# Three rounds of maxima at a time over six PSUM banks, with 24 projection matmuls between, in an attention and MLP kernel

## The chip, the cores and the metric

The kernel runs on one core of a Trainium2 chip. The metric is the device time of one execution in microseconds (us). The median of three runs of the kernel before is 1689.69 us (1689.48 to 1690.15).

## The reference

The input is layer-normed, then goes through 32-head attention (head size 16, 2048 tokens) and through an MLP; the attention's output is multiplied by a gate made of the MLP's output, and the input is added.

```python
xn = (x - mean) / sqrt(var + 1e-5)              # (2048, 512), no scale or shift
q, k, v = split(xn @ wqkv)                       # 32 heads of 16
p = softmax(q @ k.T / 4)                         # per head, 2048 x 2048
s = concat(p @ v) @ wo
h = relu(xn @ w1 + b1) ** 2                      # 1792 wide
g = silu(h @ w2 + b2)
out = x + s * g
```

## The kernel before

All matrix work is done in a 32-bit form. Where full accuracy is wanted, each factor is split in a high and a low part, and three products (high-high, high-low, low-high) are added up in one PSUM bank; `terms3` lists them. A projection tile, 128 outputs by 512 tokens with 512 inputs, is therefore 4 x 3 = 12 matmuls into one bank.

**Softmax with a true maximum.** The row maximum of the scores is found in a pass of its own. `max_mm` (L280) multiplies a block of 128 queries by 512 keys of one head into a bank of the pool `pm`, and VectorE reduces the bank to one number per query (L296). A head has 16 features, kept as three split parts in 64 rows of the array: two heads lie side by side, lane j = 0 in the rows 0 to 63 and lane j = 1 in the rows 64 to 127, so a matmul of lane 0 and one of lane 1 can run at the same time. After 64 such maxima for a unit of 512 queries and four heads (`max_end`, L300), `shift` (L324) transposes the maxima on TensorE, VectorE negates and splits them, and they go by DMA through DRAM into spare rows of the query tile `qe`, from which the second pass of scores (`exp_mm`, L1117) subtracts them inside the matmul.

**Stages.** The kernel begins with layer norm, transposes and the first projections (`ln_stats` to `ln_low`, `qk_tile`, `v_tile`). Then comes the lead (L1085 to L1114): the maxima run 24 steps ahead of the main loop. Each of the `LEAD = 24` steps g has two rounds; a round is one maximum of each lane, followed by `pump(8)`, which issues the next eight matmuls of the projections still to do (`rest`). The last matmul of a projection tile issues at once what empties its bank: for a V tile, ScalarE copies it to `vt` (L951) and a DMA stores it; for a Q or K tile, ScalarE copies it to `raw` (L934, two buffers), GpSimd splits that into `hl` (L80 and L81, three buffers), and two DMAs store it (L902). The Q and K tiles of the first column block (m divisible by 4) are instead split by ScalarE and VectorE straight out of the bank (L86, L87). Along the way `max_end` issues loads of later query tiles; step 0 loads weights, step 3 splits them, step 16 loads V and the biases, and step 17 does the first `shift`.

Then comes the main loop of 512 slots (L1268 on). Each issues matmuls of the second score pass, of the maxima 24 steps on, of the MLP or output projection, and of probabilities times V. Slots 0 and 1 take the last projection tile in two halves of six matmuls; with slot 2 the MLP begins, whose first load, `load_xc` (L469), has to wait until the projections are done, because its buffer takes their place.

**PSUM.** Eight banks: `pe` has three (tile `se`: projection tiles before the loop, second-pass scores in it), `pm` three (`pm_t`: transposes, maxima), `pd` one (`pd_t`: MLP and output projection, and the last projection tile), `pv` one (`po`: probabilities times V, in the loop alone).

**Order.** The order on TensorE is that of the Python calls, and so it is for ScalarE, VectorE and GpSimd in the lead and the loop. In the lead a scheduler orders the DMA queue of SyncE; in the loop it too follows the calls.

Of the kernel before, what the change touches and what calls it, by code (L numbers as in the profile page):

```python
# [8 lines left out]
F32 = mybir.dt.float32  # L9
# [7 lines left out]
P = 128  # L17
# [10 lines left out]
LEAD = 24  # L28
# [11 lines left out]
def kernel(  # L40
# [35 lines left out]
    def split(dst, raw, hi_act=False, lo=None):  # L76
        if hi_act:
            nc.scalar.activation(dst[0], raw, AF.Copy)
        else:
            nc.gpsimd.tensor_scalar(dst[0], raw, 1.0, 0.0, op0=ALU.mult, op1=ALU.add)  # L80
        (lo or nc.gpsimd).tensor_tensor(  # L81
            dst[1], raw, dst[0].bitcast(F32), op=ALU.subtract
        )

    def split_psum(hi, lo, ps):
        nc.scalar.activation(hi, ps, AF.Copy)  # L86
        nc.vector.tensor_tensor(lo, ps, hi.bitcast(F32), op=ALU.subtract)  # L87
# [8 lines left out]
    with ExitStack() as ph:  # L96
        kp = ph.enter_context(tc.tile_pool(name="kp", bufs=1))
        sp = ph.enter_context(tc.tile_pool(name="asp", bufs=2))
        pe = ph.enter_context(tc.tile_pool(name="pe", bufs=3, space=PSUM))
        pm = ph.enter_context(tc.tile_pool(name="pm", bufs=3, space=PSUM))  # L100
        pd = ph.enter_context(tc.tile_pool(name="pd", bufs=1, space=PSUM))
        pv = ph.enter_context(tc.tile_pool(name="pv", bufs=1, space=PSUM))
# [80 lines left out]
        def later(n, fn):  # L183
            waiting.append((now[0] + n, fn))
# [92 lines left out]

        togo = {}

        def max_mm(g, j):  # L280
            u = g // 16
            qd = u // 4
            if u not in mxs:
                mxs[u] = sp.tile([P, 16, 4], F32, name="mx")
                for i in range(2):
                    togo[u, i] = [(p, qb, kc) for p in range(2) for qb in range(4) for kc in range(4)]
            p, qb, kc = togo[u, j].pop(0)
            ps = pm.tile([P, 512], F32, name="pm_t")
            nc.tensor.matmul(  # L289
                ps,  # L290
                qms[u][p][64 * j : 64 * j + 64, qb * P : (qb + 1) * P],
                kas[qd, p][64 * j : 64 * j + 64, kc * 512 : (kc + 1) * 512],
                start=True, stop=True,
            )
            c = (2 * p + j) * 4 + qb
            return nc.vector.tensor_reduce(  # L296
                mxs[u][:, c, kc : kc + 1], ps, axis=AX.X, op=ALU.max
            )
# [21 lines left out]
        def shift_due(g):  # L320
            if late and late[0][0] <= g:
                shift(late.pop(0)[1])

        def shift(u):  # L324
            pt = pm.tile([P, 512], F32, name="pm_t")
            nc.tensor.transpose(pt[:16, :P], mxs[u], ident)  # L326
            sh = sp.tile([16, 2, P], F32R, name="sh", bufs=1)
            nc.vector.tensor_scalar(sh[:, 0], pt[:16, :P], -1.0, None, op0=ALU.mult)
            nc.vector.scalar_tensor_tensor(
                sh[:, 1], pt[:16, :P], -1.0, sh[:, 0].bitcast(F32),  # L330
                op0=ALU.mult, op1=ALU.subtract,
            )
            def keep():
                for i in range(2):
                    nc.sync.dma_start(
                        sh_d[u][:, i, :].rearrange("h (b n) -> h b n", n=P),
                        sh[:, i, :].bitcast(F32),
                    )

            def back():  # L340
                for p in range(2):
                    for i in range(2):
                        shift_rows(u, p, i)

            if in_loop:
                later(1, keep)
                later(2, back)
            else:
                keep()
                back()  # L350
# [547 lines left out]
        def qk_store(m, c, hl):  # L898
            cs = slice(c * 512, (c + 1) * 512)
            dst = q_d[m] if m < 4 else k_d[m - 4]  # L900
            for i in range(2):
                nc.sync.dma_start(dst[i, :, cs], hl[:, i].bitcast(F32))  # L902

        def qk_terms(m, c, ps):
            wq, m0 = wq_cols(m)
            ms = slice(m0, m0 + P)
            xT = xTs[c]
            return terms3(ps, [
                (lambda a, q, ko=ko: wq[q, a, ko, ms], lambda b, q, ko=ko: xT[q, b, ko])
                for ko in range(KO)  # L910
            ])

        def qk_tile(m, c, last=False):
            ps = pd.tile([P, 512], F32, name="pd_t") if last else pe.tile([P, 512], F32, name="se")
            for out_, lh, rh, first_, last_ in qk_terms(m, c, ps):
                nc.tensor.matmul(out_, lh(slice(0, P)), rh(slice(0, P)), start=first_, stop=last_)  # L916
                if not last_:
                    yield
            if last:

                hl = pools["n"].tile([P, 2, 512], F32R, name="hl")
                raw = sp.tile([P, 512], F32, name="ot", bufs=1)
                nc.scalar.activation(raw, ps, AF.Copy)
                split((hl[:, 0], hl[:, 1]), raw)
                later(6, lambda: qk_store(m, c, hl))
                yield
                return
            if m % 4 == 0:
                hl = hlp.tile([P, 2, 512], F32R, name="hl")
                split_psum(hl[:, 0], hl[:, 1], ps)  # L930
            else:
                hl = hlp.tile([P, 2, 512], F32R, name="hl")
                raw = hlp.tile([P, 512], F32, name="raw", bufs=2)
                nc.scalar.activation(raw, ps, AF.Copy)  # L934
                split((hl[:, 0], hl[:, 1]), raw)
            qk_store(m, c, hl)
            yield

        def v_tile(c, tt):
            xT = xTs[c]  # L940
            ps = pe.tile([P, 512], F32, name="se")
            ts_ = slice(tt * P, (tt + 1) * P)
            for out_, lh, rh, first_, last_ in terms3(ps, [
                (lambda a, q, ko=ko: xT[q, a, ko, ts_], lambda b, q, ko=ko: wa_t[q, b, ko, 2 * P :])
                for ko in range(KO)
            ]):
                nc.tensor.matmul(out_, lh(slice(0, P)), rh(slice(0, P)), start=first_, stop=last_)  # L947
                if not last_:
                    yield
            vt = vts[(4 * c + tt) % NVT]  # L950
            nc.scalar.activation(  # L951
                vt[:, :, :DH], ps.rearrange("p (h d) -> p h d", d=DH), AF.Copy
            )
            nc.sync.dma_start(v_d[:, c * 4 + tt, :], vt.rearrange("p h d -> p (h d)"))
            yield
# [48 lines left out]
        def pump(n):  # L1004
            for _ in range(n):
                while True:
                    todo = ahead or rest
                    if not todo:
                        return
                    if next(todo[0], todo) is not todo:  # L1010
                        break
                    todo.pop(0)
# [69 lines left out]
        pump(83)  # L1082
        warm = const.tile([P, 1], F32, name="warm")
        nc.scalar.activation(warm, eps_t, AF.Exp)
        for g in range(LEAD):  # L1085
            shift_due(g)
            for j in range(2):
                max_mm(g, j)
            pump(8)
            for j in range(2):  # L1090
                max_mm(g, j)
            pump(8)
            max_end(g)
            if g == 0:
                raw_r = [load_w("wv", 3 * P, ((D + P, 3 * P),))]
            if g == 3:
                for ko in range(KO):
                    split_w(wr_t, ko, slice(3 * P, 6 * P), raw_r[0][:, ko])
                ln.close()
                pools["v"] = ph.enter_context(tc.tile_pool(name="vp", bufs=1))  # L1100
            if g == 12:
                s1.close()
                ep = ph.enter_context(tc.tile_pool(name="ep", bufs=1))
                rot["pt"] = [ep.tile([P, 512], F32, name=f"pt{i}") for i in range(NPT)]
                pools["n"] = ph.enter_context(tc.tile_pool(name="np", bufs=1))
            if g == 16:
                load_v(0)
                nc.sync.dma_start(b1_t, b1.rearrange("(fo p) -> p fo", p=P), allow_slow_non_contiguous=True)
                nc.sync.dma_start(b2_t, b2[None, :].to_broadcast([P, D]))
            if g % 2 and g < 16:  # L1110
                c, i = divmod(g // 2, 2)
                nc.sync.dma_start(
                    xn_d[i, :, :, c * 512 : (c + 1) * 512], xTs[c][:, i].bitcast(F32)
                )  # L1114
# [211 lines left out]
```

## Time and profile before

| | us |
|---|---|
| median of three runs | 1689.69 |
| the profiled execution | 1688.97 |
| its span, first to last instruction | 1687.2 |
| TensorE busy with matmuls | 1658.8 |
| VectorE, ScalarE, GpSimd busy | 1352.7, 1192.5, 520.3 |
| the lead, from the first maximum to the loop's first | 69.35 to 187.67 |

In the profile's rows PE is TensorE's matmuls and PEld its weight loads, DVE is VectorE, ACT ScalarE, POOL GpSimd, and SPq the DMA queue that SyncE issues. A row of the timeline gives the start, the duration, the engine, the line, the operation and tile with its shape and how many instructions were merged, and in square brackets how long the engine had idled and what ended that. The end of a matmul is modelled, and matmuls overlap, so the spacing of starts tells more than a duration.

### The profile page before, as it was taken

What the parts mean: (1) busy time and instruction counts of PE and PEld (TensorE: products, weight loads), DVE (VectorE), ACT (ScalarE), POOL (GpSimd) and SP (SyncE); (2) the same over time, 40 slices, a digit from 0 to 9 for tenths busy, and PEclk for the clock granted to TensorE, in tenths of its full rate; (3) what the DMA queues carried; (4) which work ended last, traced back from release to release, by engine and by line L of the source; (5) the groups of instructions that cost most, each with busy time, mean ns of one, the idle gap of its engine ahead of it and who ended that gap; (6) DMA issues with size and microseconds to landing.
All of it is one profiled execution on the core that took longest, in us unless ns stands there. A gap on an engine that the chain in (4) does not pass through costs nothing.

```text
span 1687.2 us, 35420 instructions
## 1 busy us (share of the span) xinstructions
PE 1658.8 (98%) x13312; PEld 944.1 (56%) x13312; DVE 1352.7 (80%) x2303; ACT 1192.5 (71%) x2354; POOL 520.3 (31%) x538
## 2 busy tenths in 40 slices
PE   6999999999999999999999999999999999999998
PEld 5766566556545655565566456555655565555533
DVE  6255688888888888888888888888888888887633
ACT  7221477777777777777777777777777777776675
POOL 4335566522212321231133113211321233134322
PEclk9999999999999999999999999999999999999999
DMA  7548566435333333433343334323533352157434
GB/s 282 176 142 267 169 202 185 116 84 141 88 89 95 113 83 99 107 98 82 101 118 86 80 93 143 95 69 103 139 77 86 88 141 60 42 187 222 123 113 138
DMA packets 156316, 207.73 MB, mean 123 GB/s; under 512 B 50993, under 2 KB 70961, under 8 KB 154609
## 3 DMA queue, kind: packets, MB, share of 16 engines
q1 hardware_dynamic: 156144, 205.46, 42.5%
q8 instruction: 105, 1.72, 0.4%
q14 instruction: 67, 0.54, 0.1%
HBM read 149.04 MB, written 56.08 MB: 122 GB/s over the span
## 4 chain that ended last, share of the span: by engine, by line
PE 96%; DVE 1%; DMA 1%; ACT 1%; SPq 0%; issue 0%; DVEq 0%; ACTq 0%
PE po L362 30%; PE pm_t L289 17%; PE pd_t L236 17%; PE se L1125 12%; PE pd_t L204 9%; PE se L916 5%; PE se L947 3%; DVE mx L296 1%; PE pm_t L1125 0%; PE pm_t L816 0%; PE pm_t L326 0%; DMA xt<-in_A_x_dram 0%; DMA xc<-xn_d 0%; ACT pt L1132 0%; DMA wm<-in_A_wqkv_dram 0%
## 5 line engine op out<-in xcount | busy, mean ns | idle before, releaser
L296 DVE TENSOR_REDUCE mx<-pm_t 128x1 f32<-128x512 f32 x2048 | 1275.1, 684 | 233.4 <-PE pm_t L289 135.7
L1132 ACT ACTIVATE pt<-se 128x512 f32<-128x512 f32 x1730 | 902.4, 610 | 257.4 <-PE se L1125 225.2
L289 PE MATMUL pm_t<-ka,qm 64*128 64x512 f32 x2048 | 796.8, 423 | 3.1 <-DVE mx L296 2.9
L1125 PE MATMUL se<-qe,ka 64*128 64x512 f32 x2000 | 686.4, 402 | 0.0
L362 PE MATMUL po<-pt,v 128*32 128x512 f32 x3556 | 545.1, 605 | 0.0
L289 PEld LDWEIGHTS pm_t<-ka,qm 64*128 64x128 f32 x2048 | 352.6, 184 | 276.9 <-DVE mx L296 251.4
L1125 PEld LDWEIGHTS se<-qe,ka 64*128 64x128 f32 x2000 | 339.7, 184 | 21.0 <-issue 5.7
L236 PEld LDWEIGHTS pd_t<-xc,w1s 64*128 64x128 f32 x2352 | 292.2, 187 | 82.3 <-issue 82.2
L236 PE MATMUL pd_t<-xc,w1s 64*128 64x256 f32 x2352 | 332.3, 288 | 0.0
L236 PE MATMUL pd_t<-w2t,hT 64*128 64x512 f32 x936 | 259.9, 410 | 0.0
L236 PEld LDWEIGHTS pd_t<-w2t,hT 64*128 64x128 f32 x936 | 156.0, 184 | 73.3 <-issue 65.4
L362 PE MATMUL po<-ex,v 128*32 128x512 f32 x540 | 192.3, 605 | 0.0
L1132 ACT ACTIVATE ex<-se 128x512 f32<-128x512 f32 x270 | 147.4, 613 | 36.5 <-PE se L1125 30.8
L362 PEld LDWEIGHTS po<-pt,v 128*32 128x32 f32 x3556 | 79.9, 108 | 132.8 <-issue 112.4
L536 POOL TENSOR_TENSOR r<-r 128x512 f32<-128x512 f32 x49 | 51.1, 1042 | 329.6 <-ACT r L533 329.6
L555 POOL TENSOR_TENSOR u<-u,b_t 128x512 f32<-128x512 f32 x16 | 20.6, 1290 | 307.6 <-ACT u L554 307.6
L204 PE MATMUL pd_t<-w2t,hT 64*128 64x512 f32 x408 | 105.6, 391 | 0.0
L400 POOL TENSOR_TENSOR ot<-ot,hl 128x512 f32<-128x512 f32 x30 | 38.6, 1286 | 184.1 <-DMA hl<-r_d 184.1
L204 PE MATMUL pd_t<-wot,oc 64*128 64x512 f32 x336 | 90.9, 407 | 2.6 <-DVE m L316 0.8
L204 PEld LDWEIGHTS pd_t<-wot,oc 64*128 64x128 f32 x336 | 58.8, 185 | 47.3 <-DVE mx L296 12.4
L204 PEld LDWEIGHTS pd_t<-w2t,hT 64*128 64x128 f32 x408 | 72.8, 184 | 9.2
L533 ACT ACTIVATE r<-pd_t,b_t 128x256 f32<-128x256 f32 x98 | 41.1, 471 | 50.3 <-PE pd_t L236 50.3
(115 smaller groups left out, 1113.9 us busy)
## 6 DMA issues: line engine op xcount, KB each, us to landing
w1s<-w_d SPq DMA_DIRECT2D x196, 256.0 KB
qm<-q_d SPq DMA_DIRECT2D x384, 32.0 KB
qe<-q_d SPq DMA_DIRECT2D x384, 32.0 KB
ka<-k_d SPq DMA_DIRECT2D x96, 128.0 KB
xn_d<-xT SPq DMA_DIRECT2D x8, 1024.0 KB
k_d<-hl SPq DMA_DIRECT2D x32, 256.0 KB
q_d<-hl SPq DMA_DIRECT2D x32, 256.0 KB
xc<-xn_d SPq DMA_DIRECT2D x16, 512.0 KB
```

The costliest lines, as they stand in the source:

```text
L204: mm = nc.tensor.matmul(out_, lh(r), rh(r), start=first_ and lane == 0, stop=last_ and lane == 1, skip_group_check=True,)
L236: mm = nc.tensor.matmul(out_, lh(r), rh(r), start=first_ and lane == 0, stop=last_ and lane == 1, skip_group_check=True,)
L289: nc.tensor.matmul(ps, qms[u][p][64 * j : 64 * j + 64, qb * P : (qb + 1) * P], kas[qd, p][64 * j : 64 * j + 64, kc * 512 : (kc + 1) * 512] ...
L296: return nc.vector.tensor_reduce(mxs[u][:, c, kc : kc + 1], ps, axis=AX.X, op=ALU.max)
L362: nc.tensor.matmul(po[32 * j : 32 * j + 32, :], vs[qd][:, (4 * kb + j) * VW : (4 * kb + j) * VW + 32], pts[j], start=(kb == 0), stop=(kb = ...
L400: nc.gpsimd.tensor_tensor(ot, ot, hl[:, 1].bitcast(F32), op=ALU.mult)
L533: nc.scalar.activation(r[:, i], ps[:, i * CW : (i + 1) * CW], AF.Relu, bias=b1_t[:, fo : fo + 1])
L536: nc.gpsimd.tensor_tensor(r, r, r, op=ALU.mult)
L916: nc.tensor.matmul(out_, lh(slice(0, P)), rh(slice(0, P)), start=first_, stop=last_)
L947: nc.tensor.matmul(out_, lh(slice(0, P)), rh(slice(0, P)), start=first_, stop=last_)
L1125: nc.tensor.matmul(se, kas[qd, j // 2][b : b + 64, kb * P : (kb + 1) * P], qes[u][j // 2][b : b + 64, :], start=True, stop=True,)
L1132: return nc.scalar.activation(pts[j], se, AF.Exp, scale=0.25)
```

## The change

In the lead the rounds are no longer followed by eight matmuls each. Three rounds (six maxima) follow each other, and after every third come 24 matmuls of the projections, which are two whole tiles. The maxima of lane 0 go to the banks of `pe`, those of lane 1 to the banks of `pm`, so that six banks are in use. The projection tiles of the lead alternate between the single bank of `pd` and the single bank of `pv`. The numbers of maxima, projection matmuls and transfers are the same. The 48 rounds and 384 projection matmuls thus make 16 groups. What a step issues at its end (`max_end` and the loads) now comes after its second round and, where a group ends there, after the 24 matmuls. The first `shift` falls before the second round of a group.

```diff
-        def max_mm(g, j):
+        def max_mm(g, j, bank=None):
...
-            ps = pm.tile([P, 512], F32, name="pm_t")
+            ps = pm.tile([P, 512], F32, name="pm_t") if bank is None else bank()
...
+        led = []
+
+        def qkv_bank():
+            if not led:
+                return pe.tile([P, 512], F32, name="se")
+            led.append(0)
+            if len(led) % 2:
+                return pv.tile([P, 512], F32, name="po")
+            return pd.tile([P, 512], F32, name="pd_t")
+
         def qk_tile(m, c, last=False):
-            ps = pd.tile([P, 512], F32, name="pd_t") if last else pe.tile([P, 512], F32, name="se")
+            ps = pd.tile([P, 512], F32, name="pd_t") if last else qkv_bank()
...
         def v_tile(c, tt):
-            ps = pe.tile([P, 512], F32, name="se")
+            ps = qkv_bank()
...
-        for g in range(LEAD):
-            shift_due(g)
+        led.append(0)
+
+        for rnd in range(2 * LEAD):
+            g = rnd // 2
+            if rnd % 2 == 0:
+                shift_due(g)
             for j in range(2):
-                max_mm(g, j)
-            pump(8)
-            for j in range(2):
-                max_mm(g, j)
-            pump(8)
+                max_mm(g, j, None if j else lambda: pe.tile([P, 512], F32, name="se"))
+            if rnd % 3 == 2:
+                pump(24)
+            if rnd % 2 == 0:
+                continue
             max_end(g)
```

## The prediction

> **What bounds the kernel now.** I read the page first: the engines' busy shares and the chain of work that ended last.
>
> ```profile
> PE 1658.8 (98%) x13312; PEld 944.1 (56%) x13312; DVE 1352.7 (80%) x2303; ACT 1192.5 (71%) x2354; POOL 520.3 (31%) x538
> PE 96%; DVE 1%; DMA 1%; ACT 1%; SPq 0%; issue 0%; DVEq 0%; ACTq 0%
> ```
>
> TensorE is busy for 98% of the span and makes 96% of the chain. A microsecond saved on it anywhere should reach the end, unless something not tied to it has to be waited for. The second view is the same chain cut to the start of the lead, the third TensorE's timeline early and late in the lead.
>
> ```profile
> 55.42 11.20 PE se L947 x48
> ```
> ```profile
> 69.35 0.50 PE L289 MATMUL pm_t<-ka,qm 64*128 64x512 f32 x2
> 69.78 2.13 PE L947 MATMUL se<-wa_t,xT 128*128 128x512 f32 x8
> 71.84 0.50 PE L289 MATMUL pm_t<-ka,qm 64*128 64x512 f32 x2
> 72.27 2.13 PE L947 MATMUL se<-wa_t,xT 128*128 128x512 f32 x8
> ```
> ```profile
> 131.26 0.51 PE L289 MATMUL pm_t<-ka,qm 64*128 64x512 f32 x2
> 131.70 2.08 PE L916 MATMUL se<-xT,wr_t 128*128 128x512 f32 x8
> 133.71 0.51 PE L289 MATMUL pm_t<-ka,qm 64*128 64x512 f32 x2
> 134.14 2.08 PE L916 MATMUL se<-xT,wr_t 128*128 128x512 f32 x8
> ```
>
> Projection matmuls on the full array stream at 11.20 / 48 = 0.233 us each. In the lead a round takes 133.71 - 131.26 = 2.45 us late and 71.84 - 69.35 = 2.49 us early: 0.43 to 0.44 from the pair of maxima to the next full matmul, and 2.01 (early 2.06) for eight matmuls that would stream in 8 x 0.233 = 1.87. Nothing in these rows is a wait for another engine; what a round costs beyond streaming is the change of the array from 128 rows to two lanes of 64 and back.
>
> What a pair costs without a change of shape is seen at the loop's first slots, where pairs (one maximum, one second-pass score, in the two lanes) follow each other:
>
> ```profile
> 187.67 0.49 PE L289 MATMUL pm_t<-ka,qm 64*128 64x512 f32 x1
> 187.67 0.50 PE L1125 MATMUL se<-qe,ka 64*128 64x512 f32 x1
> 188.00 0.39 PE L289 MATMUL pm_t<-ka,qm 64*128 64x512 f32 x1
> 188.01 0.39 PE L1125 MATMUL se<-qe,ka 64*128 64x512 f32 x1
> 188.33 1.66 PE L916 MATMUL pd_t<-xT,wr_t 128*128 128x512 f32 x6
> ...
> 197.12 0.49 PE L289 MATMUL pm_t<-ka,qm 64*128 64x512 f32 x1
> ...
> 197.45 0.40 PE L289 MATMUL pm_t<-ka,qm 64*128 64x512 f32 x1
> ...
> 197.69 0.39 PE L289 MATMUL pm_t<-ka,qm 64*128 64x512 f32 x1
> ```
>
> Two pairs between full matmuls take 188.33 - 187.67 = 0.66 us, against 0.43 for one; a third adds 197.69 - 197.45 = 0.24.
>
> **The change, part by part.**
>
> *Fewer changes of shape.* The counts stay: 96 maxima and 384 projection matmuls, the same reductions, copies, splits and DMAs. A group of three rounds should take 0.66 + 0.24 = 0.90 us for its pairs, and for its 24 matmuls 2.01 + 16 x 0.233 = 5.74 (early 5.79): 6.64 late, 6.69 early. Three rounds before take 7.35 and 7.47. The early rate holds for the tiles with the first weights, nine tiles or about five groups: 5 x 6.69 + 11 x 6.64 = 106.5 us for all 16. The lead before runs from 69.35 to 187.67, 118.3 us. The difference is 11.8 us.
>
> *The first group.* Its third lane-0 maximum takes the `pe` bank of the last projection tile before the lead, which VectorE still has to read:
>
> ```profile
> 70.09 0.69 DVE L87 TENSOR_TENSOR hl<-se,hl 128x512 fp32r<-128x512 f32 x1 [13.31 <-ACT hl L86]
> 70.69 1.28 DVE L296 TENSOR_REDUCE mx<-pm_t 128x1 f32<-128x512 f32 x2
> ```
>
> It can start at about 70.8, and would otherwise at 69.35 + 0.33 + 0.24 = 69.9: TensorE loses 0.9 us, once. The six reductions behind it, at 1.28 a pair, end at 70.69 + 3 x 1.28 = 74.5, before the second group at about 76.6.
>
> *The group with the shift.* Step 17 begins with the 35th round, the second of its group. Today the transpose costs little:
>
> ```profile
> 150.84 0.51 PE L289 MATMUL pm_t<-ka,qm 64*128 64x512 f32 x2
> 151.27 2.08 PE L916 MATMUL se<-xT,wr_t 128*128 128x512 f32 x8
> 153.19 0.27 PE L326 MATMUL pm_t<-ident,m 128*16 128x128 f32 x1
> 153.39 0.50 PE L289 MATMUL pm_t<-ka,qm 64*128 64x512 f32 x2
> ```
> ```profile
> 151.37 1.29 DVE L296 TENSOR_REDUCE mx<-pm_t 128x1 f32<-128x512 f32 x2 [1.16 <-PE pm_t L289]
> ```
>
> That round takes 153.39 - 150.84 = 2.55, 0.1 more than others. Now the transpose takes a fourth `pm` bank inside a group, so the third lane-1 maximum waits for the reduction of the first. A reduction starts 151.37 - 150.84 = 0.53 after its pair and two take 1.29: the bank is free 1.8 us after the group begins, when about 0.8 would have done. With the transpose's own change of shape I take 1.2 us, once; bounds 0.1 (as today) and 2.0.
>
> *VectorE.* Six reductions take 3 x 1.29 = 3.87 us, and with 0.53 ahead of them end 4.4 us after the group begins; the next begins at 6.64. TensorE's 24 matmuls hide them with 2 us to spare, so I cost the six banks at nothing.
>
> *Two banks for projections.* Instead of three `pe` banks there are one of `pd` and one of `po`. A bank is wanted again after one other tile and three rounds: 12 x 0.233 + 0.90 = 3.7 us after its tile's end. What empties it is ScalarE, then GpSimd and the stores:
>
> ```profile
> 187.86 0.60 ACT L934 ACTIVATE raw<-se 128x512 f32<-128x512 f32 x1 [2.75 <-PE se L916]
> ```
> ```profile
> 188.54 0.63 POOL L80 TENSOR_SCALAR hl<-raw 128x512 fp32r<-128x512 f32 x1 [1.36 <-ACT raw L934]
> 189.25 1.29 POOL L81 TENSOR_TENSOR hl<-raw,hl 128x512 fp32r<-128x512 f32 x1
> ```
>
> The lead's last tile gives way to the loop's first pair at 187.67, and its copy is done at 188.46: free 0.8 us after the tile, against 3.7. GpSimd needs 190.54 - 188.54 = 2.0 us a tile and gets 6.64 / 2 = 3.3. I cost it at nothing; if ScalarE's copy came later than 3.7 us after a tile, all of the excess would fall on TensorE. The DMAs are the same in number, 10% closer together; the moves of a few query loads past stores on SyncE's queue change nobody's due time by more than a few us, and those tiles are used tens of us later. ScalarE's split of weights at step 3 now comes ahead of another tile's copy and delays it by at most its own 1.75 us, within the same slack:
>
> ```profile
> 88.97 1.75 ACT L880 ACTIVATE wr_t<-wv 128x384 fp32r<-128x384 f32 x4
> ```
>
> *After the lead.* Slots 0 and 1 find all banks free, as the last 24 matmuls come after the last maxima. What is late next is the MLP's first load:
>
> ```profile
> 193.76 1.26 SPq L472 DMA_DIRECT2D xc<-xn_d  x2
> ```
> ```profile
> PEld pd_t L204 <- DMA xc<-xn_d: 0.4, 1, 0.4
> ```
>
> It is issued when the last projection matmul is over, so it moves with the lead; TensorE waits for it 0.4 us now, and with the last stores closer together that may grow by up to 1 us. The loop behind it is TensorE's, and inherits the earlier start whole.
>
> *Sum.* 118.3 - (106.5 + 0.9 + 1.2) = 9.7 us. The profiled execution, 1688.97 us (span 1687.2 and 1.8 around it), would become 1679.3; it lies 0.7 under the median of the runs, so 1680.0 in their terms. With neither one-off loss the gain is 11.8 (1677.9); with the shift at 2.0, 1 us more at the MLP's load, and 0.2 us a group lost on the pairs (the first rival below), it is 9.7 - 0.8 - 1.0 - 3.2 = 4.7 (1685.0).
>
> **The rivals.**
>
> *The pairs do not stream as in the loop* (the change does half of what it says). Two pairs of maxima could follow at the 0.33 us of 188.00 to 188.33 instead of 0.23. Against: 197.45 to 197.69. Cost 32 x 0.10 = 3.2 us: 1683.2.
>
> *The banks set the pace.* In the loop TensorE does wait for reductions:
>
> ```profile
> 190.50 0.39 PE L289 MATMUL pm_t<-ka,qm 64*128 64x512 f32 x1
> 191.20 0.49 PE L289 MATMUL pm_t<-ka,qm 64*128 64x512 f32 x1 [0.32 <-DVE mx L296]
> ```
>
> The start comes 0.70 after the one before it, 0.47 more than streaming. If each of 16 groups had such a wait, 7.5 of the 9.7 us would be gone: 1687.5, no measurable change. For it: six banks are filled in 0.9 us and emptied in 3.9. Against it: the 5.74 us of other work between. The loop packs four maxima on three banks into a slot, without that pause. [...]
>
> *Slower: the projection banks.* If the copy out of `pd` or `po` lagged, TensorE would stand before every tile. The lag would come from behind: `hl` has three buffers, whose stores must land, and at step 16 SyncE's queue is held by the loads of V and biases. The point is a lag of 3.7 us after a tile; to lose 9.7 and 3.4 more it must be 13.1 / 16 = 0.8 us beyond, 4.5 us in all groups. At 5.0 the loss is 16 x 1.3 = 20.8: 1700.8. For it: two banks, two `raw`, three `hl`. Against: ScalarE and GpSimd wait for TensorE in these rows (2.75 and 1.36 us idle), not the other way.
>
> **How the numbers follow.** 0.2% is 3.4 us, about what a measurement of this kernel can tell from no change. Forecast as summed, 0.75, own range 1677.9 to 1682.5; pairs that do not stream, 0.11; banks set the pace, 0.08; slower, 0.06. The first two lie over 0.2% below: faster 0.86. Same 0.08, slower 0.06. The range takes in the first two with the bounds above: 1677.9 to 1685.0.
>
> **What would show it.** In the changed kernel's timeline the lead starts at about 69.4 and its groups follow every 6.6 to 6.7 us; the pairs inside start 0.33 and 0.24 apart; the first group's third pair starts near 70.9; one group late in the lead has a wait for a reduction of about 1 us; the loop's first pair starts near 178. The prediction is wrong if TensorE shows waits for L296 or for L934 in every group, or if the first MLP matmul does not come about 9.5 us earlier than now:
>
> ```profile
> 200.16 0.78 PE L204 MATMUL pd_t<-xc,w1s 64*128 64x256 f32 x2
> ```

## The result and the profile after

The changed kernel takes 1678.51 us in the median of six runs (1677.46 to 1681.39), the kernel before 1689.92 us (1689.17 to 1692.16). The ratio is 0.9937, 95% interval 0.9925 to 0.9948: 11.4 us faster, 8.8 to 12.7 by the interval. The profiled execution of the changed kernel was the slowest of its six, 1681.39 us with a span of 1679.6.

The page of the changed kernel shows the same engines at the same shares, with 12.0 us less on TensorE's matmuls:

```profile
PE 1646.8 (98%) x13312; PEld 945.2 (56%) x13312; DVE 1350.0 (80%) x2303; ACT 1192.7 (71%) x2354; POOL 519.2 (31%) x538
```

TensorE's timeline shows the first group, the second, one late in the lead, and the loop's first pair (lines of this kernel lie 12 to 16 further down: L959 is the V tiles, L928 the Q and K tiles, L1141 the second pass of scores):

```profile
69.91 0.49 PE L289 MATMUL pm_t<-ka,qm 64*128 64x512 f32 x1
...
70.25 0.39 PE L289 MATMUL pm_t<-ka,qm 64*128 64x512 f32 x1
71.39 0.50 PE L289 MATMUL se<-ka,qm 64*128 64x512 f32 x1 [0.75 <-DVE hl L87]
...
71.82 3.06 PE L959 MATMUL pd_t<-wa_t,xT 128*128 128x512 f32 x12
74.71 2.97 PE L959 MATMUL po<-wa_t,xT 128*128 128x512 f32 x12
77.61 0.49 PE L289 MATMUL se<-ka,qm 64*128 64x512 f32 x1
...
77.95 0.39 PE L289 MATMUL se<-ka,qm 64*128 64x512 f32 x1
...
78.18 0.39 PE L289 MATMUL se<-ka,qm 64*128 64x512 f32 x1
...
78.50 3.06 PE L959 MATMUL pd_t<-wa_t,xT 128*128 128x512 f32 x12
```
```profile
151.57 0.49 PE L289 MATMUL se<-ka,qm 64*128 64x512 f32 x1
...
152.46 3.01 PE L928 MATMUL pd_t<-xT,wr_t 128*128 128x512 f32 x12
...
158.12 0.49 PE L289 MATMUL se<-ka,qm 64*128 64x512 f32 x1
...
177.78 0.49 PE L1141 MATMUL se<-qe,ka 64*128 64x512 f32 x1
...
190.27 0.52 PE L204 MATMUL pd_t<-xc,w1s 64*128 64x256 f32 x2
```

Three pairs and the return to the full array take 78.50 - 77.61 = 0.89 us, 24 matmuls 158.12 - 152.46 = 5.66, a late group 6.55. The lead takes 177.78 - 69.91 = 107.9 us in place of 118.3. In this execution it began 0.56 us later than in the one before, so the first MLP matmul comes 200.16 - 190.27 = 9.9 us earlier.

The weight loads (PEld) show one place where a change of shape costs. The first two rows below are of the kernel before, whose pair starts at 131.26 and whose next full matmul at 131.70; the other two are the second pair of the changed kernel's group at 151.57:

```profile
131.26 0.18 PEld L289 LDWEIGHTS pm_t<-ka,qm 64*128 64x128 f32 x2 [0.35 <-issue]
131.69 1.66 PEld L916 LDWEIGHTS se<-xT,wr_t 128*128 128x128 f32 x8 [0.25 <-issue]
```
```profile
151.67 0.19 PEld L289 LDWEIGHTS se<-ka,qm 64*128 64x128 f32 x1
...
151.90 0.39 PE L289 MATMUL se<-ka,qm 64*128 64x512 f32 x1
```

Between pairs the weights are loaded 0.23 us ahead, under the matmul before. At both edges of a pair in the kernel before, the load starts only with its own matmul. How much of the price of a change is this load, the rows do not show.

The place of each unit's transpose on TensorE (L326) tells how far the new execution is ahead of the old one along the loop. The second, the 30th and the 31st of the 32, in the kernel before and then in the changed one:

```profile
213.77 0.28 PE L326 MATMUL pm_t<-ident,m 128*16 128x128 f32 x1
...
1500.68 0.28 PE L326 MATMUL pm_t<-ident,m 128*16 128x128 f32 x1
...
1557.49 0.28 PE L326 MATMUL pm_t<-ident,m 128*16 128x128 f32 x1
```
```profile
203.58 0.28 PE L326 MATMUL pm_t<-ident,m 128*16 128x128 f32 x1
...
1490.19 0.28 PE L326 MATMUL pm_t<-ident,m 128*16 128x128 f32 x1
...
1550.38 0.28 PE L326 MATMUL pm_t<-ident,m 128*16 128x128 f32 x1
```

It is 10.2 us ahead, then 10.5, then 7.1. The 3.4 us are lost at one place, shown by VectorE's timeline and SyncE's queue around it:

```profile
1525.81 2.49 DVE L296 TENSOR_REDUCE mx<-pm_t 128x1 f32<-128x512 f32 x4 [0.83 <-PE pm_t L289]
1532.89 0.25 DVE L386 RECIPROCAL sm<-sm 128x16 f32<-128x16 f32 x1 [4.59 <-DMA sm<-ot]
```
```profile
1524.51 2.70 SPq L134 DMA_DIRECT2D qe<-q_d  x6
1527.26 0.42 SPq L743 DMA_DIRECT2D sp_d<-s  x1
1527.72 2.75 SPq L134 DMA_DIRECT2D qm<-q_d  x6
1530.89 0.62 SPq L380 DMA_DIRECT2D sm<-ot  x1
```

VectorE stands still for 4.59 us before the reciprocal of the softmax sums of a late unit, because the DMA that brings them waits on SyncE's queue behind twelve query loads (2.70 and 2.75 us for the two times six). TensorE then waits 2.96 us for the maxima's banks, before its matmul at 1533.74. The kernel before has this wait too, 2.38 us long in its profile. The change does not make it. The 3.4 us lost there are about what this one execution lies above the median (2.9 us).

### The profile page after: what moved, and what is told of

Read it like the earlier page. It is cut to its first block, busy times and chain, and to the rows that moved or that the text cites. A ratio compares the mean times of both kernels' runs of the same rounds, so it can differ in the third digit from the quotient of the medians.

```text
span 1679.6 us, 35423 instructions
## 1 busy us (share of the span) xinstructions
PE 1646.8 (98%) x13312; PEld 945.2 (56%) x13312; DVE 1350.0 (80%) x2303; ACT 1192.7 (71%) x2354; POOL 519.2 (31%) x538
## 5 line engine op out<-in xcount | busy, mean ns | idle before, releaser
L296 DVE TENSOR_REDUCE mx<-pm_t 128x1 f32<-128x512 f32 x2000 | 1246.1, 684 | 183.8 <-PE pm_t L289 85.9
L1141 PE MATMUL se<-qe,ka 64*128 64x512 f32 x2000 | 686.8, 402 | 0.0
L1141 PEld LDWEIGHTS se<-qe,ka 64*128 64x128 f32 x2000 | 340.0, 184 | 21.6 <-issue 5.7
```

The source lines that it names most:

```text
L296: return nc.vector.tensor_reduce(mxs[u][:, c, kc : kc + 1], ps, axis=AX.X, op=ALU.max)
L1141: nc.tensor.matmul(se, kas[qd, j // 2][b : b + 64, kb * P : (kb + 1) * P], qes[u][j // 2][b : b + 64, :], start=True, stop=True,)
```

## The experiments

The theory is that of the prediction: each change of the array from 128 rows to two lanes of 64 and back costs TensorE time, and grouping removes 32 of 48; the banks only let the grouped maxima and tiles go unhindered. The prediction's rows put the price of one change at 2.45 - 0.24 - 1.87 = 0.34 us late and 2.49 - 0.23 - 1.87 = 0.39 us early: a round of before, less a streaming pair and eight streaming matmuls. The rivals are that the banks themselves save the time, and that reductions or copies take it back.

### The changed kernel again

> The changed kernel once more, to stand beside the variants on the same chip. The theory (each change of the array between full rows and two lanes costs TensorE 0.34 to 0.39 us, and 32 of 48 are gone) expects the lead to take 107.9 us from the first maximum to the loop's first, as in the profile of the changed kernel, and the time to be 9.5 to 11.5 us below the kernel before. In that profile a wait of 3.0 us for a reduction near 1530 us stood behind a DMA that brings the softmax sums; if such waits come and go with the transfers, this profile has it at another length while the lead is the same within 0.5 us.

1678.89 us, ratio 0.9943 (0.9928 to 0.9958) to the kernel before (1690.21). The lead runs from 69.15 to 177.04, 107.89 us, the same to 0.1. VectorE's longest wait for the sums was 2.1 us in this profiled execution (1678.23 us). So the lead is steady. What differs between these two executions arises late in the loop: the 30th transpose starts at 1490.19 in the one and at 1489.90 in the other, the 31st at 1550.38 and 1546.44.

### Banks alone

```diff
-            if rnd % 3 == 2:
-                pump(24)
+            pump(8)
```

> The changed kernel's banks with the old order: one round, then eight projection matmuls. The theory (the order saves, the banks only make it possible) expects the lead at 118.3 us and the time of the kernel before, within 1 us. The rival (the banks save: lane 0 and lane 1 in different pools, projections apart from the maxima) expects 8 us or more below it.

1689.25 us, ratio 1.0003 (0.9993 to 1.0013). The lead takes 187.67 - 69.34 = 118.33 us, as before to 0.01. The banks save nothing by themselves, and with one round at a time projecting into two single banks costs nothing.

### Order alone

```diff
-                max_mm(g, j, None if j else lambda: pe.tile([P, 512], F32, name="se"))
+                max_mm(g, j)
...
-        led.append(0)
-
         for rnd in range(2 * LEAD):
```

> Three rounds at a time and 24 matmuls between, in the old banks: maxima on the three of pm, projections on the three of pe. The theory expects the fourth, fifth and sixth maximum of each group to wait for the reductions of the first three, which end 1.2, 1.85 and 2.5 us after the group begins: pairs take about 2.9 us instead of 0.9, 16 x 2.0 = 32 us lost against the changed kernel, so about 21 us above the kernel before (1703 to 1718). The rival that banks do not matter expects the changed kernel's time, 1678 to 1681.

1733.65 us (two runs, 1728.79 and 1738.51), ratio 1.0265 (1.0228 to 1.0301): 44 us above the kernel before, twice what was expected. The waits are there, but they cost only a part of it. TensorE's timeline of one group and the granted clock over its 24 matmuls:

```profile
101.83 0.73 PE L289 MATMUL pm_t<-ka,qm 64*128 64x512 f32 x3
103.11 1.70 PE L289 MATMUL pm_t<-ka,qm 64*128 64x512 f32 x3 [0.55 <-DVE mx L296]
104.74 7.41 PE L959 MATMUL se<-wa_t,xT 128*128 128x512 f32 x24
```
```profile
104.74:112.08 7.34, 7.34 (x25) 5.57 (x25) 1.30 (x3) 0.60 (x1) 0.00 (x0) 0.77 0.14 47
```

The six maxima take 104.74 - 101.83 = 2.91 us, as worked out. The 24 matmuls behind them, which wait for nothing, take 7.34 us in place of 5.78: the seventh number after the stretch, the granted clock, is 0.77 there. The lead takes 164.2 us, 56 more than the changed kernel's; the waits make 16 x 2.0 = 32 us of that, the slower matmuls about 16 x 1.6 = 25. So the six banks are a condition, and without them the order costs far more than it saves.

### Two rounds at a time

```diff
-            if rnd % 3 == 2:
-                pump(24)
+            if rnd % 2 == 1:
+                pump(16)
```

> Two rounds at a time and 16 projection matmuls between, in the changed kernel's banks: 24 groups in place of 16. By the theory a group takes 0.66 us for two pairs and 2.01 + 8 x 0.233 = 3.88 (early 3.93) for 16 matmuls, 4.54 to 4.59 us; the lead takes 24 of these, 109 to 110 us, and has neither of the two single losses (no third bank is wanted in the first group, no fourth in the group of the transpose). So it is 1.2 to 2.5 us behind the changed kernel, 8 to 9 us below the kernel before. The rival, that the other banks save the time, expects no difference to the changed kernel; a rival by which only whole tiles in a row save time expects much less than 8 us.

1680.20 us, ratio 0.9943 (0.9928 to 0.9958). The lead runs from 69.70 to 178.51, 108.81 us. That is 10.0 us below the kernel before, where 8 to 9 were expected. Against the changed kernel's 1678.89 in the same comparison the 1.3 us are as expected, but less than the spread of the runs; the conclusion rests on the lead's duration. It falls by (118.33 - 108.81) / 24 = 0.40 us for each change of shape that is gone. Sixteen matmuls are a tile and a third, so the saving does not need whole tiles in a row.

### Without the two single losses

```diff
-        pump(83)
+        pump(71)
+        led += [0, 0]
+        pump(12)
...
-        led.append(0)
...
-            if rnd % 2 == 0:
+            if rnd % 3 == 0:
                 shift_due(g)
```

> The changed kernel without its two single losses: the last projection tile before the lead goes to the bank of pv, so that the first group's third maximum finds a free bank, and the transpose is issued ahead of a group instead of after its first pair. The theory expects the lead at 106.0 to 106.6 us (107.9 less 0.75 to 0.9 for the first group and 0.6 to 0.9 for the transpose), and the time 1.4 to 2.0 us below the changed kernel. The rival, that these waits are covered by something later, expects no difference.

1677.80 us, ratio 0.9935 (0.9919 to 0.9950). The lead runs from 70.11 to 175.96, 105.85 us, 2.0 less than the changed kernel's; the first group has no wait:

```profile
70.11 0.49 PE L289 MATMUL se<-ka,qm 64*128 64x512 f32 x1
...
70.45 0.39 PE L289 MATMUL se<-ka,qm 64*128 64x512 f32 x1
...
70.68 0.39 PE L289 MATMUL se<-ka,qm 64*128 64x512 f32 x1
...
71.00 3.06 PE L959 MATMUL pd_t<-wa_t,xT 128*128 128x512 f32 x12
```

Of the 2.0 us, the first group gives 1.0 (6.67 in place of 7.70 us) and the group with the transpose 0.95 (7.04 in place of 7.99). That group is still 0.5 above the others: the transpose starts 0.20 us ahead of its first pair (149.25 and 149.45), it still takes a bank of `pm`, and the third maximum of lane 1 starts 0.18 us behind that of lane 0 (150.20 and 150.02). The transpose now also comes one group later, because the next group begins two rounds after it is due.

The median is 1.1 below the changed kernel's, which these runs cannot tell from nothing. With 48, 24 and 16 groups at 118.33, 108.81 and 105.85 us, the price of a change of shape is 0.40 and (108.81 - 105.85) / 8 = 0.37 us.

### Six rounds at a time

```diff
-            if rnd % 3 == 2:
-                pump(24)
+            if rnd % 6 == 5:
+                pump(48)
```

> Six rounds at a time and 48 projection matmuls between: twelve maxima over six banks, eight groups. Fewer changes of shape would save another 8 x 0.35 = 2.8 us, but from the seventh maximum on each waits for a reduction: the pairs of a group take about 4.85 us in place of 1.6, 8 x 3.25 = 26 us. The theory expects 20 to 26 us above the changed kernel (1699 to 1704). A rival by which reductions never hold TensorE expects 2 to 3 us below it.

1715.49 us (two runs), ratio 1.0157 (1.0137 to 1.0177): 37 us above the changed kernel's 1678.89 of the other comparison instead of 20 to 26. Again the waits are as worked out, and the clock falls on top:

```profile
104.31 0.49 PE L289 MATMUL se<-ka,qm 64*128 64x512 f32 x1
...
105.58 0.49 PE L289 MATMUL se<-ka,qm 64*128 64x512 f32 x1 [0.32 <-DVE mx L296]
106.18 0.49 PE L289 MATMUL pm_t<-ka,qm 64*128 64x512 f32 x1
106.82 0.47 PE L289 MATMUL se<-ka,qm 64*128 64x512 f32 x1 [0.15 <-DVE mx L296]
...
109.30 5.49 PE L959 MATMUL pd_t<-wa_t,xT 128*128 128x512 f32 x12
```
```profile
104.31:109.30 4.99, 4.21 (x14) 1.69 (x13) 4.46 (x8) 0.60 (x1) 0.00 (x0) 0.89 0.53 172
109.30:114.58 5.28, 5.28 (x13) 4.12 (x13) 2.81 (x5) 0.00 (x0) 0.00 (x0) 0.50 0.32 114
114.58:123.06 8.48, 8.48 (x37) 6.72 (x36) 0.00 (x0) 1.79 (x3) 3.77 (x4) 0.98 0.40 134
```

The maxima take 109.30 - 104.31 = 4.99 us (4.85 expected); the next twelve matmuls take 5.28 at a granted clock of 0.50, where twelve behind the pairs of the changed kernel's first group take 74.71 - 71.82 = 2.89 at a granted clock of 1.00. In two later groups these twelve take 4.44 us each (182.59 to 187.03, 200.00 to 204.44). Of the group sizes tried, three rounds are the largest with which six banks leave TensorE no wait in an ordinary group.

### One projection bank

```diff
-            if len(led) % 2:
-                return pv.tile([P, 512], F32, name="po")
             return pd.tile([P, 512], F32, name="pd_t")
```

> The changed kernel with all projection tiles of the lead in the one bank of pd. The second tile of each group has to wait for ScalarE's copy of the first (0.2 us to its start, 0.60 long, 0.1 until TensorE goes on), the first tile of the next group finds its bank emptied behind the 0.9 us of pairs. The theory expects 16 x 0.9 = 14 us more than the changed kernel, 1690 to 1695, and thereby that the second bank hides all of that copy. If the copies lag by several us (the slower rival of the prediction), it expects 16 x 3 us or more, over 1720; if the banks are no limit, no change.

1697.53 us (two runs), ratio 1.0051 (1.0031 to 1.0071): 18.6 us above the changed kernel's 1678.89 of the other comparison, against 14 expected.

```profile
131.90 0.49 PE L289 MATMUL se<-ka,qm 64*128 64x512 f32 x1
...
132.79 3.01 PE L926 MATMUL pd_t<-xT,wr_t 128*128 128x512 f32 x12
136.57 3.02 PE L926 MATMUL pd_t<-xT,wr_t 128*128 128x512 f32 x12 [0.77 <-ACT raw L944]
139.52 0.49 PE L289 MATMUL se<-ka,qm 64*128 64x512 f32 x1
```

A group takes 139.52 - 131.90 = 7.62 us in place of 6.55, so one uncovered copy costs 1.07 us, not 0.9. The tile after the pairs does not wait. In the changed kernel neither tile waits, so the second bank hides the copy whole; copies that lag by several us are not there.

### The sums one slot later

In addition to the edits of the variant without the single losses:

```diff
-EVAC_LAST = (1, 3, 4, 5, 7, 9)
+EVAC_LAST = (1, 4, 4, 5, 7, 9)
```

> As the variant without the two single losses, and in addition the reciprocal of the softmax sums of the last four units (EVAC_LAST) is issued one slot later, so that VectorE has one slot of 3.3 us more before it meets the DMA that brings the sums. If the 3.0 us by which the changed kernel's profiled execution fell behind near 1530 us is VectorE standing in that wait, the profile here shows no wait over 1 us there, and the time is 1 to 4 us below the variant without this edit, with a smaller spread. If the wait comes from elsewhere, nothing changes.

1674.78 us (1673.47 to 1675.89), ratio 0.9913 (0.9897 to 0.9929). All its five runs lie below all six of the variant without this edit (1676.12 to 1681.61), 3.0 us in the medians, and the spread falls from 5.5 to 2.4 us. The wait for the sums, 2.8 us once late in the loop in that variant's profile, is gone there. Who waited, from 1450 to 1670 us, first without the edit and then with it:

```profile
DVE sm L386 <- DMA sm<-ot: 2.8, 1, 2.8
PE pm_t L289 <- DVE mx L296: 1.8, 3, 1.2
```
```profile
PE pm_t L289 <- DVE mx L296: 0.6, 2, 0.3
```

The transposes on either side of that place show what it is worth in the profiled executions: the one with the edit is 1.0 us ahead at the 30th (1488.14 against 1489.15) and 3.0 ahead at the 31st (1543.39 against 1546.40), so 2.0 us are gained there. The spans differ by only 0.8 us (1674.1 and 1674.9), because that execution loses 2.2 us again after the 31st. In the last of the page's 40 slices its granted clock has the digit 8 (0.8 to 0.9), without the edit the digit 9. So the end of the kernel varies too, and the 3.0 us of the medians are those of five and six runs.

This is the fastest of all kernels here: 15.4 us below the kernel before, of which 2 to 3 have nothing to do with the lead.

## Why the prediction was right

**What bounds the kernel.** Right. The lead is TensorE's: it was busy for 118.32 of its 118.32 us before and for 106.61 of 107.87 after. What it gained there (10.4 us, less the 0.56 by which that execution began it later) was still there along the loop, at 10.2 to 10.5 us from the second transpose to the wait at 1530.

**Fewer changes of shape.** Right in kind and size. The pairs take 0.89 (0.90 forecast), 24 matmuls 5.78 early (5.79) and 5.66 late (5.74, so 0.08 too much in some ten groups). The 0.08 come from the streaming rate: 0.233 us a matmul was read from tiles with the first weights and used for all, but in the late tiles 16 more matmuls add 5.66 - 2.01 = 3.65 us, 0.228 each. With 8 x 0.228 = 1.82 in place of 1.87, and 0.23 for the pair, the rows of before give 0.40 us for a change late too. The three doses, 48, 24 and 16 changes, give 0.37 to 0.40 us each.

**The first group.** Right: its third pair starts at 71.39 where 70.48 would have done, 0.91 us late (0.9). The whole group is 7.70 us long, 1.0 more than the next. (By the forecast's own numbers the second group would have begun at 69.35 + 6.69 + 0.9 = 76.9, not 76.6; nothing hangs on it.)

**The group with the shift.** In kind right, a little small: from 143.58 to 151.57 it takes 7.99 us, 1.44 more than others (1.2 forecast). TensorE's timeline shows the wait at the fourth bank:

```profile
143.58 0.50 PE L289 MATMUL pm_t<-ka,qm 64*128 64x512 f32 x1
144.01 0.28 PE L326 MATMUL pm_t<-ident,m 128*16 128x128 f32 x1
...
145.46 0.50 PE L289 MATMUL pm_t<-ka,qm 64*128 64x512 f32 x1 [0.51 <-DVE mx L296]
```

The third maximum of lane 1 starts 145.46 - 143.58 = 1.88 us after the group began (1.8 forecast), where an ordinary group has it at 0.56, and the full matmuls follow 0.43 us behind it in place of 0.33. Of the 1.44 us the variant without the single losses keeps 0.5.

**VectorE, and the rival that the banks set the pace.** Costed at nothing, rightly: VectorE idles in each ordinary group until the next one's maxima come, 2.87 us before the group at 158.12. The banks do set the pace as soon as the cover goes, with three banks or with twelve maxima: the lead then grows by 56 and 37 us, about 1.8 and 1.6 times what the waits alone were expected to cost.

**Two banks for projections, and the slower rival.** Costed at nothing, rightly; one bank costs 17 us. The copies did not lag: that of the tile in `po` which ends at 158.12 starts at 158.31 and takes 0.60 us.

**After the lead.** The wait for the MLP's first load is 0.2 us (0.4 before), not longer.

**The sum.** 9.7 us were forecast for the lead, 10.4 came; the difference is the late 24 matmuls, which took about 0.8 us less, partly offset by the group with the shift. The medians differ by 11.4 us. The last microsecond is inside the interval, and the runs don't show where it would lie; the varying wait for the sums is one candidate, the varying clock near the end another, neither proved. The upper end of the own range, 1682.5, has no working: a shift at 2.0 and 1 us more at the MLP's load give 1689.7 - 7.9 = 1681.8.

## What to carry to other kernels

When TensorE alternates between full-row matmuls and packed lanes, count the alternations, read the price of one from two neighbouring rows of the timeline (0.37 to 0.40 us here), and group the packed ones as long as PSUM banks and the work between cover their emptying; with six rounds in place of three the gain had turned into a loss, 37 us above the changed kernel. Where a group newly takes more banks, look at its edges: what held the bank last, and what else, like a transpose, draws from the same pool. Price TensorE's waits not by their length alone: look at the granted clock of the matmuls behind them (24 took 7.34 us at 0.77 with the old banks, 5.78 at 1.00 in the changed kernel).

## What the runs showed of the hardware that was not expected

In two variants, stretches with short waits are followed by a lower clock on TensorE. In the variant with the old banks the wait shown inside a group is 0.55 us, yet the granted clock over the next 24 matmuls was 0.77; over those of the changed kernel's second group (78.50 to 84.28) it was 1.00. In the 24 matmuls of the group before the one shown, it was 0.50 in an earlier stretch and 1.00 in a later one (seventh number):

```profile
95.50:98.00 2.50, 2.50 (x7) 1.91 (x7) 0.33 (x1) 0.00 (x0) 1.29 (x2) 0.50 0.00 0
98.96:101.83 2.87, 2.87 (x13) 2.07 (x12) 0.69 (x1) 0.60 (x1) 0.00 (x0) 1.00 0.42 154
```

With six rounds the clock was 0.89 during 4.99 us of maxima that came in steps of 0.6 us, then 0.50 for the following 5.28 us, and 0.98 after it (114.58 to 123.06). The granted clock from 70 to 215 us, with the old banks and with six rounds:

```profile
70.00:103.00 33.00, 29.51 (x95) 19.57 (x93) 12.96 (x22) 7.32 (x13) 3.88 (x4) 0.84 0.30 112
103.00:135.00 32.00, 29.47 (x93) 19.74 (x93) 12.44 (x22) 3.59 (x6) 5.40 (x6) 0.84 0.37 116
135.00:170.00 35.00, 32.77 (x103) 22.64 (x104) 12.67 (x21) 3.58 (x6) 11.64 (x13) 0.80 0.65 232
170.00:215.00 45.00, 41.96 (x138) 28.36 (x136) 15.63 (x28) 5.95 (x10) 17.17 (x20) 0.85 0.41 124
```
```profile
70.00:103.00 33.00, 31.60 (x111) 21.98 (x111) 14.90 (x25) 6.38 (x13) 3.86 (x4) 0.90 0.28 104
103.00:135.00 32.00, 30.41 (x103) 20.70 (x103) 14.53 (x24) 3.59 (x6) 7.48 (x8) 0.84 0.48 162
135.00:170.00 35.00, 31.61 (x112) 21.98 (x111) 15.22 (x27) 4.30 (x8) 13.59 (x17) 0.85 0.73 231
170.00:215.00 45.00, 43.35 (x168) 30.95 (x166) 15.82 (x26) 8.05 (x14) 22.34 (x24) 0.92 0.40 138
```

As an estimate, with each stretch's length times what its clock lacks to 1.00, and as if TensorE were busy throughout, that is 33 x 0.16 + 32 x 0.16 + 35 x 0.20 + 45 x 0.15 = 24 us in the first variant (145 of its lead's 164 us), where the expectation, which counted waits alone, missed 23; in the second it is 33 x 0.10 + 32 x 0.16 + 35 x 0.15 + 45 x 0.08 = 17 us, where it missed 11 to 17.

Not every variant with waits shows it. With one projection bank TensorE waits 0.77 us in the group shown above, and is idle for 125.19 - 111.20 = 14.0 us of the lead, over which its clock is 1.00:

```profile
69.06:194.25 125.19, 111.20 (x482) 77.67 (x481) 60.85 (x101) 22.27 (x38) 46.03 (x50) 1.00 0.53 180
```

There the maxima take 0.89 us a group, in the groups shown of the two variants with the lower clock 2.91 and 4.99 us. What makes the difference, these runs don't show.
